# An order of instructions in which the softmax steps of a tile go ahead, and a table of step durations brought up to date

## The chip, the cores and the metric

The kernel runs on one core of a Trainium2 chip. The metric is the device time of one execution in microseconds; the median of several runs counts. The core has five engines that work in parallel, each through its own queue in order: TensorE (PE: matrix products and transposes, into PSUM), VectorE (DVE), ScalarE (ACT), GpSimd (POOL), and SyncE (SP), which here issues the DMA transfers. An engine that reaches an instruction whose input is not there waits, and all that stands behind it in its queue waits too.

## What is computed

Attention over 2 x 8 heads, then two feed-forward stages on the 1152 rows that come out. The weights of the feed-forward stages arrive as 64-bit floating-point numbers.

```python
def _attn_ref(q, k, v):                      # 2 x 8 heads, 1152 keys, head dimension 64
    q_pool = q.reshape(B, H, S // 2, 2, D).mean(axis=3)          # 576 queries
    scores = scale * np.matmul(q_pool, k.transpose(0, 1, 3, 2))
    scores = scores - np.max(scores, axis=-1, keepdims=True)
    attn = np.exp(scores)
    attn = attn / (np.sum(attn, axis=-1, keepdims=True) + 1e-09)
    return np.matmul(attn, v)

def _moe_ref(x, w_in, w_out, a, b):          # 512 -> 2048 -> 512
    h = x @ w_in
    P = a[0] + a[1] * h + a[2] * h**2 + a[3] * h**3
    Q = 1.0 + np.abs(b[0]) * np.abs(h) + np.abs(b[1]) * h**2
    return (P / (Q + 1e-6)) @ w_out

def _moe2_ref(x, w_gate, w_val, w_out, rms_g):   # 512 -> 1536 -> 512
    xn = x / np.sqrt(np.mean(x * x, axis=-1, keepdims=True) + 1e-6) * rms_g
    g = xn @ w_gate
    return (g / (1 + np.exp(-g)) * (xn @ w_val)) @ w_out
```

## The kernel before

**Attention.** Two heads make a pair, and a pair has 9 tiles of 128 queries, so there are 72 tiles. A tile goes through a ring: TensorE computes 128 x 1152 scores into three PSUM banks (L755); VectorE takes the maximum of each row (L784, written to `nm`); ScalarE takes the exponential and its row sums (L790, `p` and `sums`); TensorE transposes `p` in blocks of 64 into the same banks (L805); ScalarE (L837) and VectorE (L840) copy the three banks to `pt` in SBUF, 512 or 128 columns at a time. Only then are the banks free for the scores of the tile after next: there are two sets of banks. Products with v (L908, `av`) run on TensorE between the scores and the transposes.

Around the ring lies other work. Each head's k and q are transposed first (L703 into `prep`, copied by L592 or L589); q is summed in pairs of rows before that (L645, `qp`, on VectorE or GpSimd). At the end of a pair 1/sum is formed (L882, L883), spread by GpSimd (L891, L893, `rx`), transposed, and multiplied into the result (L959, and L964 for the rest); the result is split into a high and a low part (L592 `x_hi`, L605 `x_lo`), which the feed-forward stage reads. Meanwhile the 64-bit weights are turned into pairs of 32-bit numbers: ScalarE L171 (and L211), VectorE L176, L180, L186 (or L219), GpSimd L215, then the high part (L199, L228) and the low part (L204, L232). 9 weights stay in SBUF; 23 are "spilled", that is, stored to DRAM as pairs (L237) and loaded again in the first feed-forward stage.

**First feed-forward stage.** 16 hidden units of 128 columns. TensorE projects (L498 into `hid`, of which there are two), then a chain of ScalarE and VectorE steps makes the rational function (L1095 to L1143: `m_u`, `m_p`, `m_q`; L1104, L1126 and L1132 are VectorE's, L1129 is GpSimd's in every second unit), and GpSimd forms the low part (L1146, `g_lo`). The first two units go in three pieces of 384 columns. The output products (L498 into `accp`, two banks) are added to `acc` by VectorE (L1201), or copied by ScalarE for the first group (L1199). The second feed-forward stage is built alike.

**What sets the order.** Nobody writes the order down. Each step is an `Op` with an engine or several to choose from (`ways`), a duration in ns (`cost`), a key (the time when it is wanted), and what it needs. `order` plays the program through: at each turn it computes for every step that is ready when it could start, takes for each engine the step with the smallest key among those that could start within `slack` ns of the earliest (80 ns in attention, 0 later), and issues the one that starts first. The durations come from tables (`S_STEPS`, `W_STEPS`, `W_OTHER`) and from `cost`, a line in the number of columns for each engine. TensorE's order of scores, transposes and products with v is tied by hand in `attention`; the preparations, and the projections of the first units, are put among them by `order`. Whatever `order` thinks of the times, on the chip only the order and the engines remain.

```python
                t0 = min(t for t, _ in c)
                picks.append(min(((op.key, op.at, t, op) for t, op in c if t <= t0 + slack))[2:])
```

Of the kernel before, what the change touches and what calls it, by code (L numbers as in the profile page):

```python
# [19 lines left out]
def attention_moe_moe2_kernel(  # L20
# [267 lines left out]
    class Op:  # L288
        def __init__(self, eng, cost, key, fn, deps=(), bufs=(), other=()):
# [39 lines left out]
    def order(slack):  # L329
# [48 lines left out]
        while ready:  # L378
# [40 lines left out]
    def cost(eng, n):  # L419
        return {PE: 0.425 * n, DVE: 70 + 1.04 * n, ACT: 60 + 0.834 * n, POOL: 148 + 2.104 * n}[eng]  # L420
# [163 lines left out]
    def copy_ways(dst, src, n, psum=False, scale=None, fast=False, seen=lambda ins: None):  # L584
# [28 lines left out]
    def head_ops(i):  # L613
# [28 lines left out]
        def f_add(eng):  # L642
# [6 lines left out]
            [(POOL, cost(POOL, m), lambda: f_add(nc.gpsimd)), (DVE, cost(DVE, m), lambda: f_add(nc.vector))],  # L649
# [85 lines left out]
    def tile_ops(i):  # L735
# [59 lines left out]
        o_exp = Op(ACT, 1430, key + 2400, f_exp, [o_red], [nb, pb, sb])  # L795
        sum_op.setdefault(pr, []).append(o_exp)
# [50 lines left out]
        for n_ in range(3):  # L847
# [7 lines left out]
            )  # L855
            if n_ == 0:
# [202 lines left out]
    def rational(u, key):  # L1059
# [19 lines left out]
        def chain(cs):  # L1079
# [70 lines left out]
            o_p1 = Op(ACT, cost(ACT, n) + 150, k + 1000, f_p1, h, [ps, bp])  # L1150
# [345 lines left out]
```

## Time and profile before

| | |
|---|---|
| median of 3 runs | 743.21 us (742.76 to 744.55) |
| profiled execution, own time | 745.6 us |
| its span, first to last instruction | 743.8 us |
| busy: PE, DVE, ACT, POOL | 699.0, 556.3, 403.4, 280.6 us |
| mean granted clock of TensorE | 0.986 of full speed |

The span is what the rows below add up to; the execution's own time has 1.8 us more around it. The share of an engine's busy time is a mean over stages. A row of waits names the engine and line that waited, and the engine and line it waited for.

### The profile page before, as it was taken

How to read it: one execution, taken by the hardware profiler on the slowest of the kernel's cores; microseconds unless marked ns; L12 is line 12 of the kernel's file. 1: busy time of each engine (PE TensorE's matmuls, PEld its weight loads, DVE VectorE, ACT ScalarE, POOL GpSimd, SP SyncE). 2: the span in 40 equal slices, each digit the busy share in tenths (PEclk: the TensorE clock that was granted, in tenths of full speed). 3: DMA queues.
4: the chain of work that ended last, by engine and by line, in shares of the span. 5: the costliest groups of instructions: out<-in, count | busy, mean ns of one | idle time of the engine just before them, and what ended most of it. 6: DMA issues, size and time to landing. Idle time of an engine off the chain costs nothing.

```text
span 743.8 us, 13108 instructions
## 1 busy us (share of the span) xinstructions
PE 699.0 (94%) x5257; PEld 604.0 (81%) x5257; DVE 556.3 (75%) x723; ACT 403.4 (54%) x633; POOL 280.6 (38%) x245
## 2 busy tenths in 40 slices
PE   8899989998998999899999899899999999999997
PEld 7666666666666668889889799798999899989996
DVE  4799998988878773987977859957769346854844
ACT  4767677677777764898745756416423222312210
POOL 3032455645455520444442352326436123612500
PEclk9999989999999999999999999999999999999999
DMA  7444465446445330223104104000224202420103
GB/s 207 117 155 129 122 214 179 161 162 234 162 150 184 129 115 28 87 85 114 58 16 155 56 1 142 29 28 1 62 82 142 85 29 85 135 93 29 57 1 127
DMA packets 51596, 77.13 MB, mean 104 GB/s; under 512 B 4176, under 2 KB 33872, under 8 KB 51536
## 3 DMA queue, kind: packets, MB, share of 16 engines
q1 hardware_dynamic: 51536, 76.30, 31.6%
q8 instruction: 41, 0.67, 0.4%
q14 instruction: 19, 0.16, 0.1%
HBM read 61.87 MB, written 14.42 MB: 103 GB/s over the span
## 4 chain that ended last, share of the span: by engine, by line
PE 62%; DVE 20%; ACT 9%; issue 6%; POOL 2%; DMA 1%; SPq 0%; DVEq 0%; POOLq 0%; ACTq 0%
PE hid L498 22%; PE accp L498 16%; PE hid L755 9%; PE av L908 8%; PE hid L805 4%; DVE nm L784 2%; DVE pt L840 2%; ACT p L790 2%; DVE m_p L1132 2%; DVE m_q L1111 1%; DVE wc L186 1%; PE prep L703 1%; DVE m_q L1126 1%; ACT m_p L1098 1%; DVE wc L180 1%
## 5 line engine op out<-in xcount | busy, mean ns | idle before, releaser
L498 PE MATMUL hid<-x_hi,win_hi 128*128 128x384 f32 x480 | 162.3, 338 | 5.8 <-issue 2.8
L498 PE MATMUL hid<-x_lo,win_hi 128*128 128x384 f32 x480 | 161.5, 336 | 0.0
L498 PE MATMUL hid<-x_hi,win_lo 128*128 128x384 f32 x480 | 161.2, 336 | 0.0
L790 ACT ACTIVATE p<-hid,nm 128x1152 f32<-128x1152 f32 x72 | 87.7, 1220 | 31.0 <-DVE nm L784 30.5
L755 PE MATMUL hid<-kT,qT 64*128 64x256 f32 (+3 forms) x800 | 99.9, 383 | 3.8 <-DVE pt L840 3.3
L784 DVE TENSOR_REDUCE nm<-hid 128x1 f32<-128x1152 f32 x72 | 94.6, 1351 | 9.6 <-PE hid L755 8.6
L498 PEld LDWEIGHTS hid<-x_hi,win_hi 128*128 128x128 f32 x480 | 90.6, 189 | 8.7 <-issue 5.6
L498 PEld LDWEIGHTS hid<-x_lo,win_hi 128*128 128x128 f32 x480 | 90.6, 189 | 1.2 <-DVE x_lo L1304 0.3
L498 PEld LDWEIGHTS hid<-x_hi,win_lo 128*128 128x128 f32 x480 | 90.7, 189 | 0.0
L755 PEld LDWEIGHTS hid<-kT,qT 64*128 64x128 f32 (+1 forms) x800 | 75.4, 185 | 14.1 <-DVE pt L840 4.7
L805 PEld LDWEIGHTS hid<-ident,p 64*128 64x128 f32 x1296 | 54.3, 143 | 37.4 <-ACT p L790 17.2
L805 PE MATMUL hid<-ident,p 64*128 64x64 f32 x1296 | 69.2, 234 | 12.5 <-ACT p L790 10.1
L1146 POOL TENSOR_TENSOR g_lo<-m_p,g_hi 128x1152 fp32r<-128x1152 f32 (+1 forms) x20 | 47.0, 2360 | 88.0 <-ACT g_hi L1143 88.0
L498 PE MATMUL accp<-g_hi,wout_hi 128*128 128x384 f32 x192 | 66.1, 344 | 11.3 <-DVE acc L1201 9.9
L908 PE MATMUL av<-pt,vn 128*64 128x288 f32 x576 | 76.7, 411 | 0.0
L837 ACT ACTIVATE pt<-hid 128x512 f32<-128x512 f32 (+2 forms) x130 | 55.7, 461 | 31.1 <-PE hid L805 28.4
L199 POOL TENSOR_SCALAR win_hi<-wc 128x512 fp32r<-128x512 f32 x25 | 16.2, 648 | 135.8 <-PE hid L498 105.6
L840 DVE COPY pt<-hid 128x512 f32<-128x512 f32 (+2 forms) x94 | 51.7, 567 | 18.4 <-PE hid L805 18.1
L498 PE MATMUL accp<-g_lo,wout_hi 128*128 128x384 f32 x192 | 64.9, 338 | 0.2 <-POOL g_lo L1146 0.2
L498 PE MATMUL accp<-g_hi,wout_lo 128*128 128x384 f32 x192 | 64.8, 337 | 0.0
L171 ACT ACTIVATE wc<-wraw 128x512 f32<-128x512 f32 x68 | 45.9, 674 | 34.7 <-POOL wout_lo L204 15.8
L908 PEld LDWEIGHTS av<-pt,vn 128*64 128x64 f32 x576 | 38.6, 136 | 26.5 <-issue 1.9
(121 smaller groups left out, 1274.0 us busy)
## 6 DMA issues: line engine op xcount, KB each, us to landing
wraw<-in_moe_w_out_dram SPq DMA_DIRECT2D x28, 512.0 KB, 3.5
far<-spill SPq DMA_DIRECT2D x23, 512.0 KB, 3.5
wraw<-in_moe_w_in_dram SPq DMA_DIRECT2D x16, 512.0 KB, 3.8
wraw<-in_moe_w_gate_dram SPq DMA_DIRECT2D x12, 512.0 KB, 3.5
wraw<-in_moe_w_val_dram SPq DMA_DIRECT2D x12, 512.0 KB, 3.9
kn<-in_k_dram SPq DMA_DIRECT2D x16, 288.0 KB, 3.9
vn<-in_v_dram SPq DMA_DIRECT2D x16, 288.0 KB, 3.8
qn<-in_q_dram SPq DMA_DIRECT2D x16, 256.0 KB, 3.1
```

The source lines that it names most:

```text
L171: nc.scalar.activation(c.bitcast(F32), wt["raw", n][:, :, 1].bitcast(F32), AF.Abs, scale=2.0**-112)
L199: eng.tensor_scalar(hi, w_float(n), 1.0, 1.0, op0=ALU.mult, op1=ALU.mult)
L498: ins = nc.tensor.matmul(dst, lhsT=a[x], rhs=b[y], start=first and i == 0 and p == 0, stop=last and i == n - 1 and p == 2,)
L755: ins = nc.tensor.matmul(ps[to, j, c:c + x1 - x0], lhsT=qT[2 * pr + h][rows, c0:c0 + to.stop - to.start], rhs=kT[2 * pr + h][rows, x0:x1], ...
L784: nc.vector.tensor_reduce(out=e["nm"], in_=scores(), op=ALU.max, axis=AX.X, negate=True)
L790: nc.scalar.activation(e["p"], scores(), AF.Exp, bias=e["nm"], scale=1.0, accum_out=sums[pr][:, t:t + 1])
L805: ins = nc.tensor.transpose(ps[:, g, c:c + 64], e["p"][rows, 128 * j:128 * j + 128], ident[rows, rows])
L837: return nc.scalar.activation(to, src, AF.Copy)
L840: return nc.vector.tensor_copy(to, src)
L908: nc.tensor.matmul(e["av", h][64 * c:64 * c + 64, 0:QW], lhsT=v_tile[2 * pr + h][:, KEYS[kt], :], rhs=pt[pr, h][:, kt, c * QW:(c + 1) * QW ...
L1132: stt(p_(), p_(), na0, u_(), op0=ALU.add, op1=ALU.mult)
L1146: eng.tensor_sub(g_(1), p_(), g_(0).bitcast(F32))
```

## The change

Three things. The durations in the tables and in `cost` are set to others, most of them longer. An `Op` gets a mark `chain`, which the maximum, the exponential and the copies of the transposes carry. And `order` gets a rule: if a marked step could start on an engine within 700 ns (`AHEAD_OF`) of the earliest start there, only steps that would end by its start plus 100 ns (`FIT`) may be taken, or, where none would, the marked steps themselves.

```diff
-            ("ACT", 660, w_abs), ("ACT", 660, w_pm), ("DVE", 450, w_shift), ("DVE", 800, w_rest_kept),
-            ("POOL", 1300, w_times),
+            ("ACT", 680, w_abs), ("ACT", 680, w_pm), ("DVE", 540, w_shift), ("DVE", 950, w_rest_kept),
+            ("POOL", 1310, w_times),
...
-        W_STEPS += [("ACT", 500, w_abs), ("DVE", 340, w_shift), ("DVE", 600, w_sign), ("DVE", 600, w_rest)]
+        W_STEPS += [("ACT", 680, w_abs), ("DVE", 600, w_shift), ("DVE", 900, w_sign), ("DVE", 800, w_rest)]
...
+    AHEAD_OF, FIT = 700, 100
...
                 t0 = min(t for t, _ in c)
+
+                due = min(((t, op.key, op.at, op) for t, op in c if op.chain and t <= t0 + AHEAD_OF), default=None)
+                if due:
+                    td = due[0]
+                    fits = [(t, op) for t, op in c if t + op.cost <= td + FIT]
+                    c = fits or [(t, op) for t, op in c if op.chain and t <= td + FIT]
+                    t0 = min(t for t, _ in c)
                 picks.append(min(((op.key, op.at, t, op) for t, op in c if t <= t0 + slack))[2:])
...
-        return {PE: 0.425 * n, DVE: 70 + 1.04 * n, ACT: 60 + 0.834 * n, POOL: 148 + 2.104 * n}[eng]
+        return {PE: 0.45 * n, DVE: 100 + 1.09 * n, ACT: 165 + 0.85 * n, POOL: 180 + 2.15 * n}[eng]
...
-            [(POOL, cost(POOL, m), lambda: f_add(nc.gpsimd)), (DVE, cost(DVE, m), lambda: f_add(nc.vector))],
+            [(POOL, cost(POOL, m), lambda: f_add(nc.gpsimd)), (DVE, 1.7 * cost(DVE, m), lambda: f_add(nc.vector))],
...
+        o_red.chain = o_exp.chain = True
...
+            done.chain = True
...
-                o_m = Op(DVE, cost(DVE, n), k + 7000, f_m, [o_exp], [bq, bu])
-            o_t = Op(DVE, cost(DVE, n) + 60, k + 3000, f_t, [o_exp, o_p3], [bp, bu])
+                o_m = Op(DVE, 1.2 * cost(DVE, n), k + 7000, f_m, [o_exp], [bq, bu])
+            o_t = Op(DVE, 1.3 * cost(DVE, n), k + 3000, f_t, [o_exp, o_p3], [bp, bu])
```

In the kernel after, lines behind the new ones have higher numbers: the maximum is L793, the copies on VectorE L850, the preparations' copies L601, the q sum L654, the spreading of 1/sum L902 and L904, the division L970 and L975.

**VectorE, between the maxima of tiles 21 and 22 and those of tiles 23 and 24.** Before, the rest of the division, two weight steps and the low part of x stand behind the last copy and ahead of the next maxima:

```order
L784 TENSOR_REDUCE nm<-hid 128x1 x2
L180 SCALAR_TENSOR_TENSOR wc<-wraw,wc 128x512
L592 TENSOR_SCALAR xt<-av 64x288 x2
L840 COPY pt<-hid 128x8x64
L959 TENSOR_TENSOR xt<-xt,prep 128x512
L964 TENSOR_TENSOR xt<-xt,rxh 64x64 x2
L186 SCALAR_TENSOR_TENSOR wc<-wraw,wc 128x512
L176 TENSOR_SCALAR wc<-wc 128x512
L605 TENSOR_TENSOR x_lo<-xt,x_hi 128x576
L784 TENSOR_REDUCE nm<-hid 128x1 x2
```

After, at the same place:

```order
L793 TENSOR_REDUCE nm<-hid 128x1 x2
L176 TENSOR_SCALAR wc<-wc 128x512
L180 SCALAR_TENSOR_TENSOR wc<-wraw,wc 128x512
L850 COPY pt<-hid 128x8x64
L186 SCALAR_TENSOR_TENSOR wc<-wraw,wc 128x512
L850 COPY pt<-hid 128x128
L601 TENSOR_SCALAR xt<-av 64x288
L850 COPY pt<-hid 128x128
L793 TENSOR_REDUCE nm<-hid 128x1 x2
L970 TENSOR_TENSOR xt<-xt,prep 128x512
```

The division follows the maxima now, its rest and the parts of x are GpSimd's, and the weight steps stand right behind the first maxima or between copies.

**GpSimd, from the last spreading of 1/sum to the first hidden unit.** `spill` is the pair of a weight that will be stored. Before:

```order
L891 TENSOR_SCALAR rx<-rinv 128x4x64 x2
L893 TENSOR_SCALAR rx<-rinv 128x128
L964 TENSOR_TENSOR xt<-xt,rxh 64x64 x2
L1129 TENSOR_TENSOR m_q<-m_q,m_u 128x384 x3
```

After:

```order
L902 TENSOR_SCALAR rx<-rinv 128x4x64 x2
L904 TENSOR_SCALAR rx<-rinv 128x128
L215 TENSOR_TENSOR wc<-wc,wraw 128x512
L228 TENSOR_SCALAR spill<-wc 128x512
L232 TENSOR_TENSOR spill<-wc,spill 128x512
L215 TENSOR_TENSOR wc<-wc,wraw 128x512
L228 TENSOR_SCALAR spill<-wc 128x512
L232 TENSOR_TENSOR spill<-wc,spill 128x512
L215 TENSOR_TENSOR wc<-wc,wraw 128x512
L228 TENSOR_SCALAR spill<-wc 128x512
L232 TENSOR_TENSOR spill<-wc,spill 128x512
L975 TENSOR_TENSOR xt<-xt,rxh 64x64 x2
```

Three spilled weights have come between; before, they were done further up.

**VectorE, in the first hidden units, which go in pieces of 384 columns.** Before:

```order
L1101 TENSOR_TENSOR m_p<-m_p,hid 128x384
L176 TENSOR_SCALAR wc<-wc 128x512
L1104 SCALAR_TENSOR_TENSOR m_p<-m_p,ncoef,hid 128x384
L1132 SCALAR_TENSOR_TENSOR m_p<-m_p,ncoef,m_u 128x384 x3
L180 SCALAR_TENSOR_TENSOR wc<-wraw,wc 128x512
L1135 SCALAR_TENSOR_TENSOR m_p<-m_q,m_p 128x384
L1111 SCALAR_TENSOR_TENSOR m_q<-m_u,absb,hid 128x384
```

After:

```order
L1112 TENSOR_TENSOR m_p<-m_p,hid 128x384
L1115 SCALAR_TENSOR_TENSOR m_p<-m_p,ncoef,hid 128x384
L1143 SCALAR_TENSOR_TENSOR m_p<-m_p,ncoef,m_u 128x384 x3
L1146 SCALAR_TENSOR_TENSOR m_p<-m_q,m_p 128x384
L1122 SCALAR_TENSOR_TENSOR m_q<-m_u,absb,hid 128x384
```

The weight steps among these rows, and three more further down, come after the two units now.

## Rows read from the trace of the kernel before

**Rows 1.** Busy time in stages: stretch, length, engines with counts, clock, DMA.

```profile
core 0: us, PE busy (x) PEld busy (x) DVE busy (x) ACT busy (x) POOL busy (x), PEclk, DMA share, GB/s
28.00:280.00 252.00, 235.79 (x2650) 167.37 (x2650) 222.24 (x327) 183.85 (x356) 117.88 (x123) 0.99 0.48 159
92.00:103.00 11.00, 8.71 (x74) 7.04 (x72) 10.35 (x14) 7.17 (x15) 7.26 (x6) 0.69 0.60 193
280.00:325.00 45.00, 40.12 (x227) 36.29 (x226) 29.85 (x47) 32.67 (x58) 13.04 (x14) 0.96 0.22 71
325.00:500.00 175.00, 163.01 (x920) 160.11 (x919) 137.60 (x122) 104.18 (x97) 65.20 (x26) 0.99 0.20 67
```

**Rows 2.** TensorE's waits, 28 to 280 us: total us, times, longest.

```profile
PE hid L805 <- ACT p L790: 5.9, 10, 2.3
PE hid L755 <- DVE pt L840: 3.3, 7, 1.1
PE hid L805 <- DVE pt L840: 1.5, 5, 0.3
```

**Rows 3.** Timeline of VectorE, 84 to 98 us: start, duration, instruction.

```profile
89.86 0.69 DVE L186 SCALAR_TENSOR_TENSOR wc<-wraw,wc 128x512 uint32<-128x512 uint32 x1
...
91.29 1.15 DVE L605 TENSOR_TENSOR x_lo<-xt,x_hi 128x576 fp32r<-128x576 f32 x1
92.36 2.61 DVE L784 TENSOR_REDUCE nm<-hid 128x1 f32<-128x1152 f32 x2
```

**Rows 4.** Timeline of TensorE, 92 to 103 us; in brackets idle time before.

```profile
95.51 1.22 PE L805 MATMUL hid<-ident,p 64*128 64x64 f32 x17 [2.29 <-ACT p L790]
```

**Rows 5.** TensorE's waits, 325 to 500 us.

```profile
PE accp L498 <- DVE acc L1201: 9.9, 7, 3.0
```

**Rows 6.** Timeline of VectorE, 420 to 429 us.

```profile
421.91 3.83 DVE L1126 SCALAR_TENSOR_TENSOR m_q<-m_q,m_u 128x1152 f32<-128x1152 f32 x1
```

**Rows 7.** Timeline of GpSimd, 418 to 429 us.

```profile
420.80 3.72 POOL L1146 TENSOR_TENSOR g_lo<-m_p,g_hi 128x1152 fp32r<-128x1152 f32 x1 [5.85 <-ACT g_hi L1143]
```

**Rows 8.** Groups of VectorE, 28 to 280 us: count, busy us, mean ns, idle before.

```profile
L219 DVE SCALAR_TENSOR_TENSOR wc<-wraw,wc 128x512 uint32<-128x512 uint32 x23 | 21.2, 924 | 0.3
L645 DVE TENSOR_TENSOR qp<-qn 128x640 f32<-128x640 f32 x5 | 5.7, 1146 | 0.7 <-issue 0.6 <-PE prep L703 0.2
```

**Rows 9.** Groups of GpSimd, whole span.

```profile
L232 POOL TENSOR_TENSOR spill<-wc,spill 128x512 fp32r<-128x512 f32 x23 | 31.1, 1361 | 1.1
L215 POOL TENSOR_TENSOR wc<-wc,wraw 128x512 f32<-128x512 f32 x23 | 30.1, 1309 | 39.6 <-ACT p L790 21.4 <-issue 6.7 <-DVE wc L219 5.1
L645 POOL TENSOR_TENSOR qp<-qn 128x640 f32<-128x640 f32 x10 | 15.5, 1546 | 17.0 <-DMA qn<-in_q_dram 7.3 <-PE prep L703 5.1 <-DVE nm L784 4.5
L228 POOL TENSOR_SCALAR spill<-wc 128x512 fp32r<-128x512 f32 x18 | 13.1, 729 | 1.4
L605 POOL TENSOR_TENSOR x_lo<-xt,x_hi 128x576 fp32r<-128x576 f32 x2 | 2.8, 1404 | 6.9 <-DVE x_hi L592 6.9
```

**Rows 10.** Spread of L219: least, median, most ns; first and last start, us.

```profile
L219 DVE SCALAR_TENSOR_TENSOR wc<-wraw,wc x23: 673/693/1705, 95.6 to 258.8; 128x512 uint32<-128x512 uint32 x23
```

**Rows 11.** Timeline of VectorE, 299.5 to 312 us.

```profile
299.90 0.42 DVE L176 TENSOR_SCALAR wc<-wc 128x512 uint32<-128x512 uint32 x1
...
302.35 0.69 DVE L180 SCALAR_TENSOR_TENSOR wc<-wraw,wc 128x512 uint32<-128x512 uint32 x1
...
309.78 0.68 DVE L186 SCALAR_TENSOR_TENSOR wc<-wraw,wc 128x512 uint32<-128x512 uint32 x1
```

**Rows 12.** TensorE's waits, 280 to 325 us.

```profile
PE hid L498 <- DVE m_p L1104: 2.0, 1, 2.0
PE accp L498 <- ACT acc L1199: 1.5, 2, 1.2
```

**Rows 13.** Timeline of GpSimd, 246 to 320 us.

```profile
280.01 0.30 POOL L893 TENSOR_SCALAR rx<-rinv 128x128 f32<-128x128 f32 x1
290.79 0.32 POOL L964 TENSOR_TENSOR xt<-xt,rxh 64x64 f32<-64x64 f32 x1 [10.48 <-ACT rxh L945]
```

**Rows 14.** Timeline of VectorE, 0 to 30 us.

```profile
5.06 0.83 DVE L645 TENSOR_TENSOR qp<-qn 128x640 f32<-128x640 f32 x1 [3.41 <-DMA qn<-in_q_dram]
```

More of the change, by code (lines that the diff above doesn't have):

```diff
@@ L297, in __init__ @@
             self.mode = None
+            self.chain = False
             self.data = {}
@@ L592, in on @@
             seen(eng.tensor_scalar(dst(), src(), by, 1.0, op0=ALU.mult, op1=ALU.mult))
-        ways = [(ACT, cost(ACT, n), on_act), (DVE, 70 + (0.52 if fast else 1.04) * n, lambda: on(nc.vector))]
+        ways = [(ACT, cost(ACT, n), on_act), (DVE, 100 + (0.62 if fast else 1.14) * n, lambda: on(nc.vector))]
         if not psum:
-            ways.append((POOL, 30 + 1.08 * n, lambda: on(nc.gpsimd)))
+            ways.append((POOL, 30 + 1.5 * n, lambda: on(nc.gpsimd)))
         return ways
@@ L605, in on @@
             eng.tensor_sub(out(), a(), b().bitcast(F32))
-        return [(POOL, cost(POOL, n), lambda: on(nc.gpsimd)), (DVE, cost(DVE, n), lambda: on(nc.vector))]
+        return [(POOL, cost(POOL, n), lambda: on(nc.gpsimd)), (DVE, 1.2 * cost(DVE, n), lambda: on(nc.vector))]
     bank = [[[] for _ in range(3)] for _ in range(2)]
@@ L1149, in chain @@
             o_abs = Op(ACT, cost(ACT, n), k, f_abs, h, [ps, bu])
-            o_p1 = Op(ACT, cost(ACT, n) + 150, k + 1000, f_p1, h, [ps, bp])
+            o_p1 = Op(ACT, cost(ACT, n) + 165, k + 1000, f_p1, h, [ps, bp])
             o_p2 = Op(DVE, cost(DVE, n), k + 2200, f_p2, [o_p1], [ps, bp])
@@ L1154, in chain @@
             o_aq = Op(ACT, cost(ACT, n), k + 2000, f_aq, [o_q], [bq])
[L1155 to L1156 removed]
+            o_ln = Op(ACT, cost(ACT, n) + 110, k + 2000, f_ln, [o_aq], [bq, bu])
+            o_exp = Op(ACT, cost(ACT, n) + 110, k + 8000, f_exp, [o_ln], [bu])
             if u in ON_POOL:
[L1158 removed]
+                o_q1 = Op(ACT, cost(ACT, n) + 100, k + 9000, f_q1, [o_ln], [bq])
                 o_m = Op(POOL, cost(POOL, n), k + 3000, f_m_pool, [o_exp, o_q1], [bq, bu])
             else:
[L1161 to L1163 removed]
+                o_m = Op(DVE, 1.2 * cost(DVE, n), k + 7000, f_m, [o_exp], [bq, bu])
+            o_t = Op(DVE, 1.3 * cost(DVE, n), k + 3000, f_t, [o_exp, o_p3], [bp, bu])
+            o_g = Op(DVE, 1.3 * cost(DVE, n), k + 8700, f_g, [o_m, o_t], [bp, bq])
             o_hi = Op(ACT, cost(ACT, n), k + 5000, f_hi, [o_g], [bp, *g])
[L1165 removed]
+            o_lo = Op(POOL, cost(POOL, n), k + 5000, f_lo, [o_hi], [bp, *g], [(DVE, 1.3 * cost(DVE, n), lambda: f_lo(nc.vector))])
             for c in cs:
```

15 lines of the change are left out of this document (5 added, 10 removed).

## The prediction

> **What bounds the kernel now.** I read the table of stages first [rows 1]. From 28 to 280 us, where nearly all of the 72 attention tiles run, TensorE is busy for 235.79 of 252 us, VectorE for 222.24, ScalarE for 183.85 and GpSimd for 117.88. TensorE has 16.2 us without work there. From 280 to 325 us, the first two hidden units, it lacks 4.9 us; from 325 to 500 us, the rest of the first feed-forward stage, 12.0 us; no term below touches the time from 500 us on. So the time is TensorE's work plus its holes, and a change of order can only move the holes and what they do to the clock.
>
> Then I read who ends TensorE's holes in attention [rows 2]. Three entries carry 10.7 us: the transposes of p wait for the exponential (5.9 us, 10 times) or for a copy (1.5 us, 5 times), the scores wait for a copy that empties their PSUM bank (3.3 us, 7 times). These are links of one ring: scores, maximum (VectorE), exponential (ScalarE), transposes, copies, next scores. The list names no wait of TensorE on GpSimd.
>
> The timeline of VectorE shows how such a hole is made [rows 3]. From 89.86 us it runs two weight steps (L186, L176) and a subtraction (L605, until 92.4 us), and only then the two maxima. No idle time is printed at the maximum: it stood in its own engine's queue. TensorE then waited 2.29 us for the exponential [rows 4], and in the 11 us around it the granted clock is 0.69 of full speed [rows 1]: with levels of 2.4 and 1.2 GHz, 62% of 11 us at the lower one, 6.8 us which do the work of 3.4.
>
> In the first feed-forward stage the hole is another one: TensorE waits 9.9 us in 7 pieces for the adds L1201 that free its output banks [rows 5]. They stand behind long VectorE steps: L1126 took 3.83 us at 421.91 [rows 6] while GpSimd ran a 3.72 us subtraction from 420.80 [rows 7].
>
> **The change, part by part.** The arithmetic and the number of instructions on TensorE stay; what moves is the order on each engine and the engine of the steps that have a choice.
>
> *Attention, the ring.* Counted over VectorE's whole order, between the last copy of one pair of tiles and the next maximum stood 31 other steps, 17 of them weight steps; now 11 and 3. The weight steps sit behind the maximum instead (41 before, 50 now), where VectorE waits for the exponential and the transposes anyway; that wait is the cover. If it is too short, the copy behind them is late, not the maximum. I let the 10.7 us shrink as the steps do, to 11/31: 6.9 us gained. Bounds: nothing, if the ring is held elsewhere, and 10.7.
>
> *The clock.* The 3.4 us above follow from one stall of the kind that goes. Another stall may lower the clock elsewhere, so I take two thirds, 2.2 us; bounds 0 and 3.4.
>
> *Engines.* VectorE loses all six of its q sums (6 x 1.146 = 6.9 us) [rows 8], five low-part subtractions and some smaller steps; GpSimd takes them: 6 x 1.546 + 5 x 1.404 = 16.3 us for the first two kinds [rows 9]. GpSimd has 134 us idle in the stage, so the load fits. By itself I cost it at nothing: VectorE's relief is what lets the ring's steps start early, and that gain is counted already.
>
> Here a cost stands against it. The spread of L219, a weight step with two inputs from SBUF, is 673 ns at the least, 693 in the median and 1705 at the most [rows 10]; its mean in attention is 924 [rows 8]. The excess over the median is 23 x 0.231 = 5.3 us, beside 117.88 us of GpSimd work. With 16.3 us more of that work it grows by 14%, 0.7 us; for the kinds not priced and the other weight steps I treble that as the upper end, 2.2 us, and take nothing, since the 6.9 us relief is larger. The Trainium skill says why (SBUF — State Buffer, "SBUF: two separate sides"): VectorE and GpSimd share one pair of ports as an exclusive lock, and a VectorE step with two SBUF inputs blocks until GpSimd's instruction ends. The trace agrees: 420.80 + 3.72 is 424.52, and the step that began at 421.91 ended 1.22 us later. A change that moves work to GpSimd buys more of these collisions; taken in full on the path, they would make the gain 2.2 us smaller.
>
> *First hidden units.* VectorE's order there had five weight steps between the 384-column steps, from 299.90 us on, L176, L180, L186 and the first two again [rows 11], 2 x 0.42 + 2 x 0.69 + 0.68 = 2.9 us; now they stand behind the last of them. The chain is serial, and TensorE waits for it (2.0 us for L1104, 1.5 for the first copies of the output) [rows 12]. I take 2.0 us, bounds 0 and 2.9.
>
> *End of attention.* Three spilled weights now stand on GpSimd between the last spreading of 1/sum (L891, L893) and the products L964 that the last division needs: 3 x (1.309 + 0.729 + 1.361) = 10.2 us [rows 9]. Before, GpSimd idled there from 280.3 to 290.8 us [rows 13]. It fits by 0.3 us; queued behind are L964, then the last x, then the first projections that use it. I take a loss of 0.5 us; bounds 0 and 3.4, one more spill's length.
>
> *First feed-forward stage.* The table's new figures for these steps are longer, so the output products come in smaller runs: besides the common closing run, before the longest were 48, 48, 48 and 36 products without projections between them, now 48, 48, 36 and 24. A run needs an add every 12 products. The 3.8 us collisions stay, as this work stays on GpSimd, and no table of means foresees them. I take a quarter of the 9.9 us, 2.5; bounds 9.9 gained and 5 lost.
>
> *Start.* The first q sum goes from VectorE (0.83 us) [rows 14] to GpSimd (1.546): 0.7 us later for the first score. I take 0.5 lost, as the transposes of k run meanwhile; bounds 0 and 0.7.
>
> The sum: -6.9 - 2.2 - 2.0 + 0.5 - 2.5 + 0.5 = -12.6 us. The profiled execution took 745.6 us (span 743.8, 1.8 around it), so it would be 733.0; the median of the runs is 743.21, 2.4 lower, and 730.6 is the prediction for it.
>
> **The rivals.** *GpSimd's queue is late (slower).* All 16 q sums now run in GpSimd's order, among weight steps that wait for other engines. If one is late, the transposes of the next head stop TensorE's own queue. The price of one such stall is that of 95.5 us: 2.3 + 3.4 = 5.7 us. Two of them (11.4) cancel the gain; from three on (17.1) the kernel is slower, 730.6 + 17.1 = 747.7. For it: 16 us or more of extra work, in order. Against: ten of the 16 ran there before and TensorE never waited for one.
>
> *The waits only move.* TensorE is at 94% of the stage; if what ends a hole is the ring's own length and not the steps in front, the 10.7 us return under another name (preparations, banks) and the clock falls elsewhere. Left are the smaller terms, -2.0 + 0.5 + 0.5, and 742.2. For it: VectorE's 88%. Against: rows 3, where the maximum waits for nothing but its queue.
>
> *More than forecast.* The adds L1201 also come in time, as the table now takes L1132 and L1126 as longer: 7.4 us beyond the 2.5, 723.2. Against it speak the collisions.
>
> **How the numbers follow.** Forecast 0.62, its own range 724 to 738 (the port's 2.2, the end's 3.4 and half of the ring's term to one side, the rest of the ring and the clock to the other). GpSimd late 0.13, waits only move 0.12, more than forecast 0.13. From 720 to 745 lies all but the far end of the last and most of the late queue, less than 2 in 10. Faster by over 0.3% (2.2 us, about what a measurement tells): 0.62 + 0.13 + 0.02 of the middle case, 0.77; within 0.3%: 0.08 of the middle case; slower: the late queue and the rest, 0.15.
>
> **What would show it.** The ring: TensorE's waits for the exponential and the copies between 28 and 280 us fall from 10.7 to some 4 us, and no 10 us stretch of attention past the first 40 us has a clock under 0.9. The hidden units: under 3.5 us of holes in their 45 us. The end: the last L964 product starts within 1 us of the copies of av. The feed-forward stage: waits for the adds between 6 and 9 us. The start: first score about 0.5 us later. I am wrong if TensorE waits on q sums or their transposes for more than 5 us, if waits on the exponential stay near 6 us with fewer steps ahead of the maximum, or if the gain sits in the feed-forward stages.

## The result and the profile after

The changed kernel takes 724.48 us in the median of 4 runs (721.57 to 725.89), the kernel before 743.3 us in its 4 runs beside it (742.76 to 744.55). The ratio, with its 95% interval, is 0.9716 [0.9686, 0.9746], and the medians are 18.8 us apart, where 12.6 were forecast. The time lies in the range of 724 to 738, half a microsecond above its lower end; the predicted 730.6 us is 6 us too high, and the parts of the sum came out differently from the whole.

The two profiled executions (745.6 and 723.87 us, both at a clock of 0.986) stand 21.7 us apart, more than the medians, because the profile of before is 2.3 us above its median here and that of after 0.6 below. All differences of stages below are between such single executions. First the table of stages of the kernel after: stretch, length, busy time of each engine with its instructions, clock, DMA.

```profile
core 0: us, PE busy (x) PEld busy (x) DVE busy (x) ACT busy (x) POOL busy (x), PEclk, DMA share, GB/s
28.00:265.00 237.00, 231.94 (x2646) 166.58 (x2644) 206.24 (x307) 180.53 (x341) 126.85 (x136) 0.99 0.48 156
92.00:103.00 11.00, 10.72 (x110) 7.75 (x112) 9.07 (x13) 7.07 (x16) 5.37 (x5) 0.85 0.29 79
265.00:310.00 45.00, 39.77 (x209) 35.82 (x210) 32.44 (x50) 34.78 (x62) 22.34 (x23) 0.89 0.34 117
310.00:486.00 176.00, 171.45 (x980) 170.66 (x979) 143.75 (x137) 109.02 (x107) 66.97 (x31) 0.99 0.22 72
```

Attention ends 14 to 15 us earlier, so these stretches answer to those of [rows 1] shifted by as much. In 237 us of attention TensorE lacks 5.1 us, where it lacked 16.2. In the first hidden units it lacks 5.2 us in 45, where it lacked 4.9. In the rest of the first feed-forward stage 4.6 us, where it lacked 12.0. So the holes of attention and of the stage went, and those of the first hidden units stayed.

TensorE's waits after, 28 to 265 us (total us, times, longest):

```profile
PE hid L815 <- ACT p L799: 3.4, 3, 1.6
PE hid L815 <- DVE pt L850: 0.4, 2, 0.2
PE hid L764 <- ACT pt L847: 0.2, 1, 0.2
PE hid L764 <- DVE pt L850: 0.2, 1, 0.2
```

Beside [rows 2]: the exponential kept 3.4 of its 5.9 us, in 3 places, and the copies 0.8 of 4.8. The list is complete: no wait on GpSimd. And it lacks entries that the prediction had not priced, the rest of the list of before behind [rows 2] (28 to 280 us), where TensorE stops at the preparations of the next heads (L703) and at a transpose for the division (L941), 4.1 us in all:

```profile
PE prep L703 <- issue: 1.1, 1, 1.1
PE prep L703 <- PE hid L805: 0.9, 1, 0.9
PE av L941 <- DVE xt L592: 0.8, 2, 0.4
PE prep L703 <- ACT kT L589: 0.7, 1, 0.7
PE prep L703 <- DVE kT L592: 0.6, 2, 0.5
```

To compare kernels I cut each span at four events of TensorE: the first score product, the first projection of a hidden unit, the first output product, the first transpose for the normalisation behind the first feed-forward stage. Before they stand at 7.7, 279.5, 307.6, 506.5 us and the end at 743.8; after at 8.7, 265.1, 293.2, 485.8 and 722.0. That gives attention 271.8 and 256.4 us, hidden units 28.1 and 28.1, stage 198.9 and 192.6, rest 237.3 and 236.2. This is where the 21.8 us of the span come from: +1.0 at the start, -15.4 in attention, 0, -6.3 in the stage, -1.1 behind it.

The same cuts for all kernels that ran. "Waits" are TensorE's from 28 us to the end of attention, as listed by the profile; "adds" are its waits for VectorE's adds into the output's sum in the stage; the last column is the median of the runs.

| kernel | attention | waits | hidden units | stage | adds | time |
|---|---|---|---|---|---|---|
| before | 271.8 | 15.0 | 28.1 | 198.9 | 9.9 | 743.3 |
| e1, rule only | 264.4 | 10.7 | 26.5 | 203.4 | 9.9 | 741.58 |
| e2, durations only | 269.0 | 12.5 | 27.1 | 197.0 | 3.2 | 738.1 |
| e4, stage's durations old | 254.6 | 4.0 | 29.0 | 198.5 | 6.5 | 729.13 |
| e5, stage's durations new | 269.5 | 16.6 | 28.3 | 191.2 | 2.7 | 737.15 |
| e7, rule and engine factors | 263.0 | 8.1 | 27.0 | 202.0 | 10.1 | 738.27 |
| e8, rule and weight tables | 262.2 | 8.0 | 39.9 | 198.4 | 7.6 | 744.71 |
| e11, rule and lines of `cost` | 263.2 | 8.4 | 28.3 | 199.5 | 4.0 | 738.0 |
| e6, without engine factors | 257.7 | 6.1 | 27.8 | 195.5 | 3.5 | 727.84 |
| e10, without weight tables | 258.3 | 6.3 | 27.4 | 198.6 | 3.2 | 732.28 |
| e13, copies not ahead | 258.1 | 5.8 | 26.7 | 196.9 | 3.2 | 727.81 |
| after | 256.4 | 4.2 | 28.1 | 192.6 | 2.0 | 724.48 |
| e9, first q sum back | 256.1 | 4.2 | 28.0 | 192.5 | 2.0 | 722.81 |
| e12, adds go ahead too | 255.1 | 4.0 | 28.0 | 194.4 | 0.4 | 724.22 |

How far apart two executions of one attention order lie is seen in three pairs: 271.8 and 269.5 (before, e5), 256.4 and 254.6 (after, e4), 256.4 and 256.1 (after, e9, all but one q sum). Differences of 1 to 2 us in that column are near the noise.

Part of that noise is TensorE's clock. Of the attention of before, 13.7 us ran at the lower of its two levels (1.2 GHz); of e5, with the same order, 3.4. In e5 the stall that the prediction started from is there with the same 2.29 us, and the clock of the 11 us around it is 1.00, where it was 0.69 before [rows 1, 4]. Timeline of TensorE in e5, and the row of the stretch, with the clock behind the five busy times:

```profile
93.94 0.78 PE L805 MATMUL hid<-ident,p 64*128 64x64 f32 x17 [2.29 <-ACT p L790]
92.00:103.00 11.00, 7.83 (x95) 5.43 (x95) 10.85 (x14) 8.81 (x16) 7.08 (x6) 1.00 0.55 172
```

The lower level takes 13.7 us of attention in e2, 10.2 in e1, e7, e8 and e11, 6.8 in after and e9, and 3.4 in e4, e6, e10, e12 and e13. If half of that is lost time (an estimate from these traces), attention without it is 265 and 268 us with the old order, 259 in e1, 262 in e2, 257 to 258 in e7, e8 and e11, 256 to 257 in e6, e10 and e13, and 253 in after, e4, e9 and e12.

### The profile page after: what moved, and what is told of

Read it like the earlier page. It is cut to its first block, busy times and chain, and to the rows that moved or that the text cites. A ratio compares the mean times of both kernels' runs of the same rounds, so it can differ in the third digit from the quotient of the medians.

```text
span 722.0 us, 13129 instructions
## 1 busy us (share of the span) xinstructions
PE 694.9 (96%) x5257; PEld 605.0 (84%) x5257; DVE 542.4 (75%) x706; ACT 402.2 (56%) x620; POOL 299.7 (42%) x275
## 4 chain that ended last, share of the span: by engine, by line
PE 88%; DVE 4%; ACT 4%; issue 1%; DMA 1%; SPq 0%; POOL 0%; POOLq 0%; DVEq 0%; ACTq 0%
PE hid L507 33%; PE accp L507 23%; PE hid L764 11%; PE av L919 10%; PE hid L815 7%; PE prep L712 3%; ACT p L799 2%; DVE nm L793 2%; ACT pt L847 1%; PE prep L966 1%; DMA wout_lo<-far 1%; DMA qn<-in_q_dram 1%; DVE win_lo L204 0%; ACT m_u L1106 0%; ACT m_q L1125 0%
## 5 line engine op out<-in xcount | busy, mean ns | idle before, releaser
L793 DVE TENSOR_REDUCE nm<-hid 128x1 f32<-128x1152 f32 x72 | 95.1, 1353 | 9.5 <-PE hid L764 8.8
L764 PE MATMUL hid<-kT,qT 64*128 64x256 f32 (+3 forms) x800 | 98.1, 379 | 0.6 <-ACT qT L598 0.2
L764 PEld LDWEIGHTS hid<-kT,qT 64*128 64x128 f32 (+1 forms) x800 | 73.6, 180 | 11.7 <-issue 1.6
L815 PE MATMUL hid<-ident,p 64*128 64x64 f32 x1296 | 66.8, 231 | 9.0 <-ACT p L799 7.8
L1157 POOL TENSOR_TENSOR g_lo<-m_p,g_hi 128x1152 fp32r<-128x1152 f32 (+1 forms) x20 | 44.1, 2211 | 69.4 <-ACT g_hi L1154 69.4
L199 POOL TENSOR_SCALAR win_hi<-wc 128x512 fp32r<-128x512 f32 x26 | 18.2, 698 | 123.0 <-PE hid L507 104.1
L850 DVE COPY pt<-hid 128x512 f32<-128x512 f32 (+2 forms) x97 | 50.9, 541 | 22.6 <-PE hid L815 21.1
```

The lines of the kernel that those rows point to most:

```text
L199: eng.tensor_scalar(hi, w_float(n), 1.0, 1.0, op0=ALU.mult, op1=ALU.mult)
L764: ins = nc.tensor.matmul(ps[to, j, c:c + x1 - x0], lhsT=qT[2 * pr + h][rows, c0:c0 + to.stop - to.start], rhs=kT[2 * pr + h][rows, x0:x1], ...
L793: nc.vector.tensor_reduce(out=e["nm"], in_=scores(), op=ALU.max, axis=AX.X, negate=True)
L815: ins = nc.tensor.transpose(ps[:, g, c:c + 64], e["p"][rows, 128 * j:128 * j + 128], ident[rows, rows])
L850: return nc.vector.tensor_copy(to, src)
L1157: eng.tensor_sub(g_(1), p_(), g_(0).bitcast(F32))
```

## The experiments

**Rule or durations (e1, e2).** The change has two halves. e1 takes the kernel before and adds the rule and the marks:

```diff
+    AHEAD_OF, FIT = 700, 100
...
+                due = min(((t, op.key, op.at, op) for t, op in c if op.chain and t <= t0 + AHEAD_OF), default=None)
...
+        o_red.chain = o_exp.chain = True
...
+            done.chain = True
```

e2 is the changed kernel without the lines of the rule, so only the durations are new.

> The rule alone, all durations as before. Ahead of the next maximum stand 28 steps on VectorE (7 of them weight steps), after the last copy; before it were 31 (17), in the changed kernel 11 (3). Theory A, the rule makes the gain in attention because it clears weight steps out of the way: TensorE's waits on the exponential and the copies between 28 and 280 us fall from 10.7 to some 5 us and the time is 730 to 734. Theory B, the new durations and the work they send to GpSimd make it: waits stay above 8 us, 739 to 743. Theory C, neither does it without the other: 736 to 741 here and in the run with the durations alone.

> The durations alone, without the rule. Ahead of the maximum stand 14 steps (12 of them weight steps); all 16 q sums are GpSimd's. Theory A: attention gains little, waits of 8 us or more, and only the first feed-forward stage gains its 6 us, 735 to 739. Theory B: attention gains nearly what the changed kernel gains, waits under 6 us, 724 to 729. Theory C: 733 to 738, with attention between both.

Measured: e1 741.58 us, ratio 0.9953 [0.9936, 0.9969]; e2 738.1 us, 0.9899 [0.9872, 0.9926]. Against the mean of the two executions of the old attention order (270.6 us), the rule alone shortens attention by 6.2 us, the durations alone by 1.6, both together (mean of after, e4 and e9, 255.7) by 14.9; with the clock taken off as above it is some 7, 4 and 13.5. The medians of the runs, which average over the clock, say it more surely: by the ratios the rule alone takes off 3.5 us, the durations alone 7.5, both 21.1. Neither half is enough, as theory C says, though by their times e1 lies in B's range and e2 in A's. TensorE's waits in e1, 28 to 272 us:

```profile
PE hid L815 <- ACT p L799: 6.9, 7, 2.4
PE hid L815 <- DVE pt L850: 2.6, 9, 0.5
PE hid L764 <- ACT pt L847: 0.6, 3, 0.2
PE hid L764 <- DVE pt L850: 0.6, 2, 0.4
```

The waits at preparations and division are gone already, the ring's are not. Why not, the timeline of VectorE in e1 shows (150 to 161 us: start, duration, instruction, in brackets idle time before and what ended it):

```profile
153.83 0.70 DVE L219 SCALAR_TENSOR_TENSOR wc<-wraw,wc 128x512 uint32<-128x512 uint32 x1
155.08 1.83 DVE L614 TENSOR_TENSOR x_lo<-xt,x_hi 128x576 fp32r<-128x576 f32 x1 [0.56 <-POOL x_hi L601]
156.84 2.61 DVE L793 TENSOR_REDUCE nm<-hid 128x1 f32<-128x1152 f32 x2
```

Order lets the low part L614 go ahead because, by the old line, it takes 70 + 1.04 x 576 = 669 ns. On the chip it first waited 0.56 us for GpSimd and then took 1.83 us, where the shortest of its four there takes 0.76. GpSimd in e1, 153 to 158 us, ran beside it:

```profile
155.02 1.28 POOL L215 TENSOR_TENSOR wc<-wc,wraw 128x512 f32<-128x512 f32 x1
```

This ended at 156.30, and the low part 0.61 us later, as the prediction read the port [rows 6, 7]. The maxima behind it are late, and TensorE waits 2.39 us until 159.59; the same three rows stand at 222 to 225 us, with 2.39 us until 227.97. These two are 4.8 of e1's 6.9 us. After, at the same place, the low part is GpSimd's and the maxima follow the copy (VectorE, 150 to 161 us):

```profile
153.74 0.29 DVE L850 COPY pt<-hid 128x128 f32<-128x128 f32 x1 [0.64 <-PE hid L815]
154.12 2.70 DVE L793 TENSOR_REDUCE nm<-hid 128x1 f32<-128x1152 f32 x2
```

In these two places, then, the rule let a step go ahead because it took its duration for too short.

**Attention or stage (e4, e5).** e4 has the changed kernel's order up to the end of attention and the old durations from the first hidden unit on; e5 the reverse. In e4 the hidden units' steps are costed by the old lines, in e5 by the new ones:

```diff
+    def cost2(eng, n):
+        return {PE: 0.425 * n, DVE: 70 + 1.04 * n, ACT: 60 + 0.834 * n, POOL: 148 + 2.104 * n}[eng]
...
-            o_t = Op(DVE, 1.3 * cost(DVE, n), k + 3000, f_t, [o_exp, o_p3], [bp, bu])
+            o_t = Op(DVE, cost2(DVE, n) + 60, k + 3000, f_t, [o_exp, o_p3], [bp, bu])
```

> Rule and durations as in the changed kernel up to the end of attention (the order on every engine there is the same), the old durations from the first hidden unit's chain on. If the first feed-forward stage gains by its own durations: first projection at 265 us as in the changed kernel, the waits for the adds near 10 us again, 728 to 732. If the stage gained only because attention left it in another state: waits of 2 to 4 us, 723 to 726.

> The opposite: the order of before up to the end of attention, the new durations from the first hidden unit's chain on. If the stages gain by their own durations: 736 to 739, first projection at 279 us, waits for the adds of 2 to 5 us. If not: 741 to 745 and waits for the adds near 10 us.

Measured: e4 729.13 us, 0.9781 [0.9765, 0.9798]; e5 737.15 us, 0.9901 [0.9877, 0.9926]. By the ratios attention's part is 16.3 us and the stage's 7.4, together 23.6, where the change has 21.1 (0.0284 x 743.3): the parts add up within their noise. In e5 the stage is 191.2 us with the old attention in front of it, in e4 198.5 with the new one. The stage's gain is its own. The waits for the adds are 6.5 us in e4, where near 10 were expected, and 2.7 in e5.

**Which of the durations (e7, e8, e6, then e10, e11).** e7 adds to e1 only the two factors that decide the choice of engine, e8 adds only the tables of weight steps; e6 takes the two factors out of the changed kernel:

```diff
-        return [(POOL, cost(POOL, n), lambda: on(nc.gpsimd)), (DVE, cost(DVE, n), lambda: on(nc.vector))]
+        return [(POOL, cost(POOL, n), lambda: on(nc.gpsimd)), (DVE, 1.2 * cost(DVE, n), lambda: on(nc.vector))]
...
-            [(POOL, cost(POOL, m), lambda: f_add(nc.gpsimd)), (DVE, cost(DVE, m), lambda: f_add(nc.vector))],
+            [(POOL, cost(POOL, m), lambda: f_add(nc.gpsimd)), (DVE, 1.7 * cost(DVE, m), lambda: f_add(nc.vector))],
```

> The rule, and of the new durations only the two factors that make VectorE dear for the q sum (1.7) and the low part of x (1.2); all else as before. All 16 q sums go to GpSimd and 10 steps (4 of them weight steps) stand ahead of the next maximum. Attention is counted from the first score to the first projection: 271.8 us before, 256.4 in the changed kernel, 264.4 with the rule alone, 269.0 with the durations alone. Theory D, the rule needs VectorE relieved of steps that a choice of engine can take away: attention 255 to 259 and 729 to 734 in all. Theory E, the rule needs true durations of the weight steps to judge what fits: 262 to 266 here, 739 to 743 in all.

> The rule, and of the new durations only those of the weight steps (three tables). 10 q sums on GpSimd as before, 29 steps (7 of them weight steps) ahead of the next maximum, seven spilled weights on GpSimd behind the last spreading of 1/sum. Theory D: attention 262 to 266 us, and the spills make the end late; 740 to 746 in all. Theory E: attention 255 to 259; 730 to 736 in all.

> The changed kernel without the two factors, so that 5 of the 16 q sums and 4 of the 8 low parts are VectorE's again; 17 steps (6 of them weight steps) ahead of the maximum. Theory D: attention 260 to 265 us, 729 to 733 in all. Theory E: 255 to 258, 724 to 727.

Measured: e7 738.27 us, 0.9903 [0.9877, 0.9929], attention 263.0; e8 744.71 us, 0.9986 [0.9964, 1.0008], attention 262.2; e6 727.84 us, 0.9777 [0.9741, 0.9813], attention 257.7. Neither part alone supplies what the rule lacks: e7's attention speaks against D, e8's against E, and both theories that named one part missed.

e8 is no faster than before although its attention is 7 to 10 us shorter. GpSimd in e8, 268 to 312 us:

```profile
271.38 1.77 POOL L215 TENSOR_TENSOR wc<-wc,wraw 128x512 f32<-128x512 f32 x1
...
290.74 1.26 POOL L232 TENSOR_TENSOR spill<-wc,spill 128x512 fp32r<-128x512 f32 x1
...
297.70 1.27 POOL L232 TENSOR_TENSOR spill<-wc,spill 128x512 fp32r<-128x512 f32 x1
```

ScalarE in e8, 284 to 296 us:

```profile
292.04 0.67 ACT L171 ACTIVATE wc<-wraw 128x512 f32<-128x512 f32 x1 [4.66 <-POOL spill L232]
...
293.44 1.52 ACT L1106 ACTIVATE m_u<-hid,absb 128x384 f32<-128x384 f32 x3
```

And the longest of TensorE's waits in e8, 270 to 310 us:

```profile
PE hid L507 <- DVE m_p L1115: 10.6, 1, 10.6
```

Seven spilled weights stand between the last spreading of 1/sum and the first hidden units' product on GpSimd. The fifth of them ends at 292.0 us; a weight step on ScalarE has waited 4.66 us for it, and the first step of the hidden unit, L1106, stands behind that step in ScalarE's queue. So TensorE waits 10.6 us, the clock is at its lower level for 13.7 us from 293.2 on, and the hidden units last 39.9 us, 11.8 more than before. The prediction feared late spills too, but for the product L964 on GpSimd; in e8 they come through ScalarE.

e10 takes the weight tables out of the changed kernel, e11 adds to e1 only the new lines of `cost` and of the copies:

```diff
-        return {PE: 0.425 * n, DVE: 70 + 1.04 * n, ACT: 60 + 0.834 * n, POOL: 148 + 2.104 * n}[eng]
+        return {PE: 0.45 * n, DVE: 100 + 1.09 * n, ACT: 165 + 0.85 * n, POOL: 180 + 2.15 * n}[eng]
```

> The changed kernel with the durations of the two tables of weight steps put back (rule, lines of cost, factors of the engine choice as changed). Attention is counted from the first score product to the first hidden-unit product: before 271.8 us, after 256.4 us. F (the lines of cost, with ScalarE 105 ns longer, carry what the rule alone leaves): attention 255 to 259 us, TensorE's waits on the exponential and the copies at most 6 us, time 722 to 729 us. G (no single part carries it, each helps some): attention 259 to 262 us, waits 5 to 8 us, time 727 to 733 us. If the weight steps are what the rule lacks: 263 us or more, waits over 8 us, 733 us or more.

> The kernel before with the rule and only the new lines of cost (one for each engine) and of the copies; the weight steps, the factors 1.7 and 1.2 and the chain of the hidden units as before. The rule alone had 264.4 us of attention and 10.7 us of waits on the exponential and the copies. F (the lines of cost carry the rest): attention 255 to 258 us, waits at most 6 us, time 728 to 736 us. G (each part helps some): attention 259 to 263 us, waits 6 to 9 us, time 733 to 740 us. If the lines matter nothing in attention: 263 us or more.

Measured: e10 732.28 us, 0.9826 [0.9799, 0.9853], attention 258.3 and waits 6.3; e11 738.0 us, 0.9908 [0.9877, 0.9939], attention 263.2 and waits 8.4. e10's attention lies in F's range, its waits and its time in G's; e11 speaks against F and lies on the border between G and no effect. The row of numbers is G's: the rule alone 264.4 us; with one of three parts 263.0, 262.2, 263.2; with two 257.7 (lines and weights) and 258.3 (lines and factors); with all three 255.7. The third pair, factors and weights, was not run. One part gains 1.2 to 2.2 us, hardly more than the noise, the second 4.5 to 5.5, the third 2 to 2.6. The large second step is mostly the clock (10.2 us at the lower level in e7, e8 and e11, 3.4 in e6 and e10); without it, by the estimate above, the steps are 1 to 2, 1 to 2 and 3 to 4 us. What the new lines of `cost` do shows in e11's waits, 28 to 271 us:

```profile
PE hid L815 <- ACT p L799: 5.9, 8, 1.3
PE hid L815 <- DVE pt L850: 0.9, 4, 0.2
```

The longest wait is 1.3 us where e1 had 2.4, but there are eight where e1 had seven.

**Which marks (e13).** The changed kernel without the mark on the copies of the transposes:

```diff
-            done.chain = True
```

> The changed kernel in which only the maximum and the exponential go ahead, not the copies of the transposes. If the maximum and exponential carry the gain of the rule (the prediction's ring step speaks of the next maximum): attention 255 to 259 us, time within 3 us of the changed kernel's 724.5 us. If the copies need it as much, since a transposes' copy holds up the av products: attention 260 to 266 us, TensorE's waits on the copies of the transposes over 2 us (0.8 us after), time 728 to 735 us.

Measured: 727.81 us, 0.9767 [0.9736, 0.9799]; attention 258.1, waits on the copies 2.3 us. Attention lies in the first theory's range and the copies' waits in the second's; the time, 3.3 us above the changed kernel's, lies between the two. The maximum and the exponential carry most of the rule; the copies may carry 2 to 3 us of it, but the intervals of this run and of the change still touch.

**The first q sum (e9).** The changed kernel with the first head's sum of q on VectorE again:

```diff
+            [(DVE, cost(DVE, m), lambda: f_add(nc.vector))] if i == 0 else
             [(POOL, cost(POOL, m), lambda: f_add(nc.gpsimd)), (DVE, 1.7 * cost(DVE, m), lambda: f_add(nc.vector))],
```

> The changed kernel with the first head's q sum on VectorE. The order is the same but for this step. If the first sum on GpSimd costs the start what the trace shows: first score at 7.7 us in place of 8.7, and 723 to 724 where the changed kernel has 724.5; if the start is made up for later, no difference.

Measured: 722.81 us, 0.9697 [0.9669, 0.9725]. The lowest median of all, though the interval overlaps that of the change. The first score starts at 8.2 us, half a microsecond later than expected, because q landed later (below).

**The adds (e12).** e9, with the adds into the output's sum marked too:

```diff
                     yop[o, c] = Op(eng, cost(eng, CW), k + ADD, f_add, [mm, yop.get((o, c))], [ps])
+                    yop[o, c].chain = True
```

> The changed kernel with the first head's q sum back on VectorE (722.8 us) and VectorE's and ScalarE's adds into the output's sum counted among the steps that go ahead too. If TensorE's last wait for such an add (2.0 us in one place) is one of order, it goes and the time is 719 to 722 us. If nothing but the add's own length holds it, or attention's order is shifted by it: 722 to 727 us.

Measured: 724.22 us, 0.9734 [0.9707, 0.9761], no better than e9. TensorE's waits in e12, 293 to 520 us:

```profile
PE accp L507 <- ACT g_hi L1155: 5.4, 2, 3.6
PE accp L507 <- POOL g_lo L1158: 2.8, 2, 2.2
...
PE accp L507 <- DVE acc L1213: 0.4, 2, 0.3
```

The wait for the adds falls from 2.0 to 0.4 us, as the first theory had it. But waits on the hidden units' results rise from 2.4 (1.8 and 0.6 in e9, as after) to 8.2 us, and the stage is 1.9 us longer, most of it by the clock (10.2 us at the lower level in the stage, 6.8 in e9). That an add that goes ahead delays the chain that feeds the next products fits these rows; it was not tested by itself.

## Why the prediction was right, and where its steps were not

**The ring, -6.9.** The mechanism is right, and so is the size, but the size by luck. TensorE's waits on the exponential and the copies fell from 10.9 us (from 28 us to the end of attention) to 4.2, 6.7 less. But "I let the 10.7 us shrink as the steps do, to 11/31" doesn't hold. In e1 the steps ahead of the next maximum fall from 31 to 28 and the weight steps among them from 17 to 7, and the waits are 10.7. In e7 there are 10 steps, fewer than after, and 8.1 us. In e8 there are 29 and 7.2 us. Which step stands ahead and how long it lasts tells more: in e1 one L614 of 1.83 us at the wrong place makes a hole of 2.39.

**A term that was missing, -4.1.** TensorE's waits at the preparations and the division were 4.1 us of its 16.2 us without work; the prediction read the list for the ring only. Since e1, with the rule alone, has none, and e2, with the durations alone, has 2.9 us, it is the rule that removes them. With this and the ring, 10.8 of attention's 15.4 us are explained; the clock has 3.4 more.

**The clock, -2.2.** The stall remains, shorter. Timeline of TensorE after, 84 to 98 us:

```profile
90.59 0.78 PE L815 MATMUL hid<-ident,p 64*128 64x64 f32 x17 [1.58 <-ACT p L799]
```

And of VectorE after, in the same stretch:

```profile
87.39 0.29 DVE L850 COPY pt<-hid 128x128 f32<-128x128 f32 x1 [0.15 <-PE hid L815]
87.77 2.70 DVE L793 TENSOR_REDUCE nm<-hid 128x1 f32<-128x1152 f32 x2
90.39 0.68 DVE L970 TENSOR_TENSOR xt<-xt,prep 128x512 f32<-128x512 f32 x1
```

The division L970 stands behind the maxima now, as the order had it, and the maxima follow the copies; the hole of 2.29 us [rows 4] is 1.58. Before, the clock is 0.76, 0.50, 0.50 and 0.54 in the four stretches of 2 us from 94 to 102, 6.8 us at the lower level; after it is 0.95, 0.50 and 0.70 in three from 90 to 96, 3.4 us. That gives back 1.7 us, close to the term, but not because the stall went: "no 10 us stretch past the first 40 us under 0.9" failed (0.83 from 88 to 98 us). TensorE's busy time in attention fell by 3.3 us (235.3 to 231.9); 1.6 of these I can't place. In the first 28 us the lower level falls from 6.8 to 3.4 us too, for nearly the same work (203 and 205 products), another 1.7 us.

But over the whole execution this term came to nothing. What attention got back, the first feed-forward stage lost: in it the lower level takes 10.2 us, where it took 3.4. The clock falls at 303.4 us, where TensorE waits 1.8 us and then 0.6 for the second hidden unit's results. The stretch from 302 to 312 us after:

```profile
302.00:312.00 10.00, 7.97 (x28) 7.21 (x29) 8.40 (x9) 10.00 (x14) 4.23 (x4) 0.66 0.15 52
```

In all 20.5 us of either execution are at the lower level, and both have a mean clock of 0.986. "Another stall may lower the clock elsewhere" came true in full. Nor does the clock follow from the length of one stall: the 2.29 us one left it alone in e5, and of e1's two of 2.39 us the first lowered it (0.69 from 159 to 170 us) and the second did not (1.00 from 227 to 238).

**Engines and port, 0.** GpSimd's queue, the rival with 0.13, did not come: TensorE waits for a q sum once, 0.9 us at the start. The collisions grew about as the sum had it. L219's mean in attention fell from 924 ns [rows 8] to 826, but the other two weight steps with two inputs rose. Groups of VectorE, before (28 to 280 us), then after (28 to 265):

```profile
L180 DVE SCALAR_TENSOR_TENSOR wc<-wraw,wc 128x512 uint32<-128x512 uint32 x9 | 6.9, 769 | 0.0
L186 DVE SCALAR_TENSOR_TENSOR wc<-wraw,wc 128x512 uint32<-128x512 uint32 x9 | 6.8, 752 | 0.1
L219 DVE SCALAR_TENSOR_TENSOR wc<-wraw,wc 128x512 uint32<-128x512 uint32 x20 | 16.5, 826 | 0.3
L186 DVE SCALAR_TENSOR_TENSOR wc<-wraw,wc 128x512 uint32<-128x512 uint32 x9 | 9.1, 1014 | 0.0
L180 DVE SCALAR_TENSOR_TENSOR wc<-wraw,wc 128x512 uint32<-128x512 uint32 x9 | 7.9, 876 | 0.2
```

Over the median of 693 ns the three take 6.5 us too long before and 7.2 after, beside 117.88 and 126.85 us of GpSimd work. TensorE's waits fell all the same, and the upper end of 2.2 us was not needed.

**First hidden units, -2.0.** This term failed: 28.1 us before and after. The weight steps are gone from VectorE's order there, but TensorE's wait on L1115 is 1.9 us where it was 2.0 [rows 12]. The time of that wait, in the timeline of TensorE before (295 to 326 us), shows why:

```profile
299.67 0.51 PE L498 MATMUL hid<-x_hi,win_hi 128*128 128x384 f32 x1 [1.98 <-DVE m_p L1104]
```

It was over at 299.67 us, and the first of the five weight steps started at 299.90 [rows 11]: they stood behind the wait, not in it. The other 1.5 us are ScalarE's copies. "TensorE waits for it" was read as if the weight steps made that wait. "Under 3.5 us of holes" failed with it (5.2 in 45 us, 4.9 before).

**End of attention, +0.5.** Right. GpSimd after, 262 to 294 us:

```profile
276.38 1.30 POOL L232 TENSOR_TENSOR spill<-wc,spill 128x512 fp32r<-128x512 f32 x1
277.63 0.71 POOL L975 TENSOR_TENSOR xt<-xt,rxh 64x64 f32<-64x64 f32 x2
```

And VectorE after, 276 to 290 us:

```profile
277.25 0.69 DVE L970 TENSOR_TENSOR xt<-xt,prep 128x512 f32<-128x512 f32 x1 [4.04 <-ACT xt L598]
278.38 0.46 DVE L601 TENSOR_SCALAR x_hi<-xt 128x576 fp32r<-128x576 f32 x1 [0.44 <-POOL xt L975]
```

The last spill ends as the product starts, and VectorE waits 0.44 us. e8 shows what four spills more cost here.

**First feed-forward stage, -2.5.** Undersized: -6.3, though the clock took some 3.4 us more there, and the waits for the adds are 2.0 us and not 6 to 9. TensorE's waits after, 293 to 486 us:

```profile
PE hid L507 <- issue: 2.8, 2, 2.5
PE accp L507 <- DVE acc L1212: 2.0, 1, 2.0
PE accp L507 <- ACT g_hi L1154: 1.8, 1, 1.8
```

The step that failed is "the 3.8 us collisions stay [...] and no table of means foresees them". The group of L1143, 1152 columns wide, on VectorE after, 293 to 485 us (count, busy us, mean ns, idle before):

```profile
L1143 DVE SCALAR_TENSOR_TENSOR m_p<-m_p,ncoef,m_u 128x1152 f32<-128x1152 f32 x14 | 24.6, 1757 | 2.5 <-ACT m_u L1134 2.4
```

And the same group before, where it is L1132, 307 to 506 us:

```profile
L1132 DVE SCALAR_TENSOR_TENSOR m_p<-m_p,ncoef,m_u 128x1152 f32<-128x1152 f32 x14 | 29.6, 2114 | 5.9 <-ACT m_u L1123 5.9
```

Fourteen undisturbed ones would take 14 x 1.42 = 19.9 us (the median is 1.42 in both); the excess falls from 9.7 to 4.7 us, in 6 and in 4 of the 14 steps, and the longest is 2.79 us where it was 3.80. With the old durations behind the new attention (e4) the group takes 30.8 us, with the new ones behind the old (e5) 26.5.

The sum of the collisions is not the measure either: in e8 the group takes 26.4 us, as in e5, and the waits for the adds are 7.6 us where e5 has 2.7. Nor are the smaller runs that the prediction counted: e5's longest have 48, 48, 48 and 48 products, more than before. What the rows show is the place of a step that was hit: shortly ahead of an add that TensorE needs. Before, VectorE, GpSimd and TensorE at 466 to 471 us:

```profile
466.61 3.80 DVE L1132 SCALAR_TENSOR_TENSOR m_p<-m_p,ncoef,m_u 128x1152 f32<-128x1152 f32 x1
466.47 2.72 POOL L1129 TENSOR_TENSOR m_q<-m_q,m_u 128x1152 f32<-128x1152 f32 x1 [0.33 <-ACT m_q L1120]
470.93 0.69 PE L498 MATMUL accp<-g_hi,wout_hi 128*128 128x384 f32 x1 [2.98 <-DVE acc L1201]
```

The add starts when L1132 has ended. Three more of the waits before have such a step ahead: 2.78 us at 427.59 (L1126 of 3.83 us [rows 6]), 1.35 at 375.88 (L1132 of 3.36) and 1.52 at 489.59 (the weight step L186 of 3.04). The four are 8.6 of the 9.9 us. After, the one wait of 2.0 us has no such step ahead, only steps of up to 1.42 us. e8's two longest waits again stand behind such steps (2.78 us behind 3.83, 2.03 behind 2.69). That the place decides is read from these rows; no run moved one such step by itself.

The Trainium skill (SBUF — State Buffer, "SBUF: two separate sides") says that a VectorE step with two SBUF inputs and a GpSimd step that reads SBUF need one pair of ports, which the step that starts first holds for its whole instruction while the other blocks. The trace agrees for the three 1152-column steps among the four: each ended 1.22 us after a GpSimd instruction that had started first.

The adds are not all of the stage: e10 has 3.2 us of waits for adds and a stage of 198.6 us, because TensorE lacks work elsewhere there (5.7 us under "issue", that is, on nothing that the profile shows) and has 10.2 us at the lower clock level.

**Start, +0.5.** The first score starts 1.0 us later. Kernels with this sum on GpSimd have it at 8.4 to 8.9 us, those with it on VectorE at 7.7 to 8.2, 0.7 us apart in the mean, which is the upper bound given. The rest goes with the landing of q: the sum could start at 5.65 us after, at 5.84 in e9, with the sum on VectorE again, and at 5.06 before [rows 14].

The sum by measured sizes: -6.7 - 4.1 - 3.3 in attention behind 28 us, about -1 ahead of it, 0 in the hidden units, -6.3 in the stage, +1.0 at the start and -1.1 behind the stage, 21.5 of 21.8 us. So the forecast was right in its direction, by the ring and the stage. The larger misses add up on one side (a missing term of -4.1, a stage 3.8 us better than its term; against them 2.0 us of hidden units that gave nothing), and the time lies at the very end of the range. That it still lies inside is luck: what the bounds of the ring (3.8) and of the clock (1.2) leave beyond their terms makes 730.6 into 725.6, not into the 724 that was written, and the time is 724.48. The rival "more than forecast" was half right (the adds), and "the waits only move" describes e1's ring, which kept its 10.7 us with the rule alone, and the clock. A third of the gain sits in the feed-forward stage, which the prediction had named as a sign of a wrong reason; for the stage it was one, for attention not.

## What to carry to other kernels

A rule that holds a queue free for an urgent step works far better on durations that it can trust: here the rule alone took 3.5 us off the median, the new durations alone 7.5, both 21.1. Read each filler's longest time under contention from the trace, not its count or mean, and look at the single step that stands ahead of the late one. Work moved out of one place must be followed to where it lands: seven weights that came late cost e8 all that its attention had gained. And look at the clock of a whole execution, and of a second one, before a stall's price is put into a sum.

## What the hardware showed beyond that

The runs of one and the same kernel follow its mean clock closely. The changed kernel's four runs are 721.57 us at 0.992, 723.87 at 0.986, 725.09 at 0.983 and 725.89 at 0.982: 4.3 us for a hundredth of the clock. A difference of 2 us between two profiles can be that alone.

The same step can be the surer choice on the slower engine: L614 took 0.76 to 1.83 us in its four executions on VectorE in e1, and 1.40 to 1.42 in its four on GpSimd.
